# Zeroing the output during attention, smaller routing steps in expert 0, and gates kept in another buffer

## The chip, the cores and the metric

The kernel runs on one core of one Trainium2 chip. The metric is the device time of one execution in microseconds (us); the time before is the median of three runs. A core has a TensorE (PE: matmuls; PEld: its weight loads), a VectorE (DVE), a ScalarE (ACT), a GpSimd (POOL) and a SyncE (SP), which run their own instruction streams in order and wait for each other by semaphores. Transfers issued by SP and by POOL are carried out by 16 DMA engines.

## The reference

Two stages. The first is linear attention with a decaying state, over batch 4, 8 heads, 768 steps, head size 48; for each batch and head:

```
for t: cur = outer(u*k[t], v[t]);  y[t] = r[t] @ (state + cur);  state = w*state + outer(k[t], v[t])
```

The second is a mixture of experts over the 3072 rows x of 384 numbers that y makes: noisy logits for 8 experts, the two largest chosen for each row, their gates a softmax of the two, and

```
noisy = x@w_gate + log1p(exp(x@w_noise))*noise;  top2, gates = softmax over the two largest
out[row] += gate * (relu(x[row] @ w1[e]) @ w2[e])      # 384 -> 1024 -> 384, for both experts e of a row
```

## The kernel before, in words

**Attention** runs over 24 tiles (`for i in range(NT)`, L1223) of 128 rows, 6 chunks of time by 4 batches. In a tile SP loads k, r and v of tile i+4 (`load`, L139) and stores the tile's x to DRAM (`xout`, L485, into `xd`, whose last 8 columns are for the gates); PE makes transposes, scores, y (`intra`, L467; `back`, L476) and, for the tiles before, the logits (`logits`, `logits_b`, L511 to L524).

**Routing** is done by the generator `route(g)` for two groups of rows, tiles 0 to 12 and 13 to 23: some 70 small VectorE steps, among them matmuls on PE for prefix sums (L757) and for a list product (`drop`, L617), which turns one-hot matrices (L604 to L613) into the list of rows for one expert. `one(g, 1)` makes the list for expert 1, `places` and `half` those for experts 2 to 7. The steps are handed out by `rstep(us, pe)`: each call adds `us` to a credit and runs steps of the first one or two generators in the queue while credit is left; a step costs 0.2 unless it yields another price. A step that yields "pe" has a matmul next, which is let go only after a number of `rstep` calls with `pe` true. What is handed out this way stands in the engines' streams between the other work, in this order, for good.

**Experts** come in chunks of up to four tiles of 128 gathered rows: chunk (0,0), (0,1), (1,0) and so on. `xT` transposes gathered rows on PE (L1048), copies them on ACT (L1050: xh, the rounded part) and takes the remainder on DVE (L1051: xl). `p1` makes h for f = 0 to 7 in 9 matmuls each (L1075), copied by ACT (L1079) and DVE (L1081) out of a ring of three PSUM buffers; `p2` makes the output tiles in 24 matmuls each (L1111). Chunk (0,0) uses only rows of the first group, and so starts while the second group is being routed: after each f of p1(0,0) stands one `rstep(STEPS_P1)`, after every 8 matmuls of p2(0,0) one `step00`, which holds an `rstep(STEPS_P2)` and, from step 7 on, the transposes of chunk (0,1), whose rows are gathered (L977) once the second group's list for expert 0 is there. `poll` starts what has become possible: gathers, loads of gates, tokens. If the second group's gates are ready by step AT_ONE, `one(1,1)` is pushed there, else behind p2(0,0). `zero_out` writes 192 rows of zeros to the output (L1295, 16 times), since experts later add to it by gathering and scattering rows (L986, L1132); it stands in the f-loop of p1(0,0) and in `step00`. Then the attention's buffers are freed (`att_stack.close()`), and p1(0,1) begins, with `rstep(0.6)` after each f.

Of the kernel before, what the change touches and what calls it, by code (L numbers as in the profile page):

```python
# [29 lines left out]
STEPS_KV = 0.35  # L30
# [2 lines left out]
FILL = 1  # L33
STEPS_END = 0.9
FLAG_AT = 17
STEPS_P1 = 1.0
STEPS_P2 = 1.4
STEPS_P1B = 0.6
STEPS_P2B = 1.25
WARM1 = 2  # L40
# [5 lines left out]
CV_DVE = 1  # L46
POOL_LATE = 13
BIG = 3.0e38
AT_ONE = 5
NOT = 4  # L50


# [1 line left out]
def kernel(  # L54
# [14 lines left out]
    nc = tc.nc  # L69
    B, H, S, D = r.shape  # L70
    N, E = noise.shape
    DM = H * D
# [55 lines left out]
    def load(i, part=(0, 3)):  # L128
        c, b = divmod(i, B)
        for nm, src, dst in (("kt", k, kt), ("rt", r, rt), ("vt", v, vt))[part[0]:part[1]]:  # L130
            if nm == "rt":
                t = rd[i % NLD][:, :, :D]
            elif nm == "vt":
                t = vd[i % NLD][:, :, :D]
            elif i:
                t = att.tile([128, H, D], F32, name=nm, bufs=NLD - 1)
            else:
                t = kd[0][:, :, :D]
            nc.sync.dma_start(t, src[b, :, c * C:(c + 1) * C, :].rearrange("h t e -> t h e"))  # L139
            dst[i] = t  # L140

    load(0, (0, 2))
    ub = const.tile([128, H, D], F32, name="ub")
# [13 lines left out]
    zrow = const.tile([128, DM], F32, name="zrow")  # L157
# [209 lines left out]
    def prep_k(i, eng=None):  # L367
        for h in (slice(0, H // 2), slice(H // 2, H)):
            (eng or nc.gpsimd).tensor_mul(kd[i % 3][:, h, :D], kt[i][:, h], tabk[:, h, :D])  # L369
# [13 lines left out]
    def uterm_b(i):  # L383
        c8 = att.tile([128, H, 1], F32, name="c8")
        nc.vector.tensor_reduce(c8, RKU[i][:, :, :D // 2 if i > POOL_LATE else D], AX.X, ALU.add)  # L385
        C8[i] = c8
        if i <= CV_DVE:
            CV[i] = att.tile([128, H, D], F32, name="cv")
            nc.vector.tensor_mul(CV[i], vt[i], c8.to_broadcast([128, H, D]))
# [82 lines left out]
    def back(i):  # L472
        pt = psum.tile([128, 2, 2, 2, 64], F32, name="ptb", tag="py1")
        for s in range(2):
            for q in range(2):
                nc.tensor.transpose(pt[:, s, q].rearrange("p j d -> p (j d)"), YB[i][:, s, q, :], ident)  # L476
        PY[i] = pt

    def xout(i):
        x = xs[i % 2]  # L480
        nc.vector.tensor_add(x[:, :DM].rearrange("p (q j s d) -> p (q j) s d", q=2, j=2, s=2),
                             PY[i].rearrange("p s q j d -> p (q j) s d")[:, :, :, :D],
                             CV[i].rearrange("p (q j s) d -> p (q j) s d", q=2, j=2))
        X[i] = x
        nc.sync.dma_start(xd[i * 128:(i + 1) * 128, :], x)  # L485
# [31 lines left out]
    def logits_b(i):  # L517
        if i not in PL:
            return
        pl, ys, m = PL.pop(i)  # L520
        g = [i >= a for a, _ in GROUPS].count(True) - 1
        j = i - GROUPS[g][0]
        nc.tensor.transpose(pl[:, 1, :32 * m], ys[:32 * m], ident[:32 * m, :32 * m])
        nc.scalar.activation(LG[g][:, j - m + 1:j + 1, :],  # L524
                             pl[:, 1, :32 * m].rearrange("p (a b) -> p a b", b=32)[:, :, :2 * E], AF.Copy)
# [32 lines left out]
    def T_of(n):  # L558
        def T(nm, shape=(128, n, E), dt=F32, bufs=1):
            w_ = 1  # L560
            for z in shape[1:]:
                w_ *= z
            mx = w_ // n * GB
            t = att_pool[0].tile([128, mx], dt, name="r_" + nm, bufs=bufs)
            ax = "abcd"[:len(shape) - 1]
            return t[:, :w_].rearrange(f"p ({' '.join(ax)}) -> p {' '.join(ax)}",
                                       **dict(zip(ax, shape[1:])))
        return T
# [98 lines left out]
    def route(g, lists=True):  # L667
        i0, i1 = GROUPS[g]
        n = i1 - i0
# [3 lines left out]
        T = T_of(n)  # L673
# [13 lines left out]
        def P(k, shape=(128, n, E)):  # L687
            w_ = shape[1] * (shape[2] if len(shape) == 3 else 1)
            v = base[:, k * pw:k * pw + w_]
            return v.rearrange("p (a b) -> p a b", b=E) if len(shape) == 3 else v  # L690

        a, ee, zp = P(0), P(1), T("zp")
# [9 lines left out]
        d, s, s2, q, nl, sn = T("n"), P(0), P(2), T("q"), P(0), P(1)  # L702
# [92 lines left out]
        if lists:  # L795
            og = T("os", [128, 2, n, E])
            nc.vector.tensor_mul(og, oh, gts[:, :, :, None].to_broadcast([128, 2, n, E]))
            yield 0.3
            gd = T("a")
            nc.vector.tensor_add(gd, og[:, 0], og[:, 1])  # L800
            nc.sync.dma_start(xd[i0 * 128:i1 * 128, DM:].rearrange("(n p) e -> p n e", p=128), gd)
            yield 0.25
# [355 lines left out]
    def push(*gens, alone=False):  # L1158
        route_q.extend([x, 0, alone] for x in gens)

    def rstep(us, pe=True):

        credit[0] = min(credit[0] + us, us + 0.5)
        if pe:
            for it in route_q[:pairs[0]]:
                it[1] = max(it[1] - 1, 0)
        j = 0
        while j < min(pairs[0], len(route_q)):
            it = route_q[j]
            if it[1] > 0 or (it[2] and j):  # L1170
                j += 1
                continue
            if credit[0] <= 0:
                return
            try:
                c = next(it[0])
            except StopIteration:
                route_q.pop(j)
                j = 0
                continue  # L1180
            if c == "pe":
                it[1] = gap[0]
                credit[0] -= 0.3
            else:
                credit[0] -= c or 0.2
# [32 lines left out]
    def route_when_done(i):  # L1218
        for g, (a, b) in enumerate(GROUPS):
            if b == i + 1:  # L1220
                push(route(g))

    for i in range(NT):  # L1223
        nxt = i + 1 < NT
        if i == 0:
            load(NLD - 1)
        if nxt:
            trans(i + 1, 0)
            uterm_b(i + 1)
            trans(i + 1, 1)  # L1230
        kvup(i)
        inter(i)
        if i > 1:
            logits(i - 2)
        if i + 2 < NT:
            prep_k(i + 2)
            uterm_a(i + 2)
        rstep(STEPS_A, False)
        if i == I_EARLY:
            until(routed, 0)  # L1240
        poll()
        if i == FLAG_AT:
            flag = consts_c()
        if i in (FLAG_AT, FLAG_AT + 2):
            next(flag)
        if not nxt:
            until(gated, 0)
            x00 = xT(0, 0)
            p1a = p1(0, 0, True)
        zadd(i)  # L1250
        intra(i)
        if i > 1:
            logits_b(i - 2)
            route_when_done(i - 2)
        if nxt:
            uterm_c(i + 1, 0, CV_AT)
            scores(i + 1)
            mask(i + 1, 0)
        if i and nxt:
            xtrans(i - 1)  # L1260
        if nxt:
            uterm_c(i + 1, CV_AT, H)
        if not nxt:
            next(x00)
        if i + NLD < NT:
            load(i + NLD)
        if i + 1 in W0_AT:
            w_load(0, W0_AT.index(i + 1))
        back(i)
        xout(i)  # L1270
        if nxt:
            mask(i + 1, 1)
        if i - W_LAG in W0_AT:
            w_hi(0, W0_AT.index(i - W_LAG))
        if i - W_LAG - 1 in W0_AT:
            w_lo(0, W0_AT.index(i - W_LAG - 1))
        rstep(STEPS_KV if nxt else STEPS_END)
    xtrans(NT - 2)
    rstep(STEPS_END)
    next(x00)  # L1280
    xtrans(NT - 1)
    for _ in x00:
        pass
    rstep(STEPS_END)
    logits(NT - 1)
    rstep(STEPS_END)
    fill(FILL)
    pairs[0] = 2
    logits_b(NT - 1)
    route_when_done(NT - 1)  # L1290
    zq = [0]

    def zero_out():
        if zq[0] < N:
            nc.sync.dma_start(out[zq[0]:zq[0] + 192, :].rearrange("(p two) d -> p two d", two=2),  # L1295
                              zrow[:96, None, :].to_broadcast([96, 2, DM]))
            zq[0] += 192

    for whole in p1a:
        if whole:  # L1300
            zero_out()
            rstep(STEPS_P1)
            poll()

    at00 = [0]

    def step00():
        zero_out()
        at00[0] += 1
        rstep(STEPS_P2)  # L1310
        poll()
        if 1 in gated and at00[0] <= AT_ONE and "one" not in did:
            did.add("one")
            push(one(1, 1))
        if "rest" in did and at00[0] > 6:
            next(x01, None)
# [4 lines left out]
    for t in p2(0, 0, step00):  # L1321
        next(wl, None)
        hold.append((0, t))
    while zq[0] < N:
        zero_out()
    until(routed, 1)
    until(gated, 1)
    while route_q:
# [94 lines left out]
    with tc.If(any_r > 0):  # L1423
        bad_r = nc.values_load(tab[:, E:E + 1], min_val=0, max_val=1)
        with tc.If(bad_r > 0):
# [12 lines left out]
            for i in range(NT):  # L1438
                c, b = divmod(i, B)
# [20 lines left out]
        for kk in range(2):  # L1460
# [3 lines left out]
            for i in range(NT):  # L1464
                nc.gpsimd.indirect_dma_start(
                    out=lst, out_offset=bass.IndirectOffsetOnAxis(ap=SLI[:, kk, i:i + 1], axis=0),
# [32 lines left out]
```

## Time and profile before

| what | value |
|---|---|
| time, median of 3 runs | 612.76 us (612.59 to 614.89) |
| profiled execution: its own time, its span | 614.7 us, 612.9 us |
| busy PE, PEld, DVE, ACT, POOL | 577.1, 539.8, 363.3, 252.8, 272.3 us |
| PE in the chain that ended last | 77% of the span (p1's L1075 30%, p2's L1111 29%) |
| mean granted TensorE clock | 0.986 of full speed |
| attention tiles 16 to 23 | about 103 to 147 us of the span |
| p1(0,0), p2(0,0) | 152.8 to 166.4, 166.4 to 185.6 us |
| p1(0,1), p2(0,1) | 186.5 to 206.7, 206.7 to 226.1 us |

Busy time of an engine says little by itself, as the stages have different limits; a row of the timeline gives start, duration, engine, line, operation, output <- inputs, shapes, the number of instructions merged and, in brackets, the idle time of the engine before and what ended it.

### The profile page before, as it was taken

How to read it: one execution, taken by the hardware profiler on the slowest of the kernel's cores; microseconds unless marked ns; L12 is line 12 of the kernel's file. 1: busy time of each engine (PE TensorE's matmuls, PEld its weight loads, DVE VectorE, ACT ScalarE, POOL GpSimd, SP SyncE). 2: the span in 40 equal slices, each digit the busy share in tenths (PEclk: the TensorE clock that was granted, in tenths of full speed). 3: DMA queues.
4: the chain of work that ended last, by engine and by line, in shares of the span. 5: the costliest groups of instructions: out<-in, count | busy, mean ns of one | idle time of the engine just before them, and what ended most of it. 6: DMA issues, size and time to landing. Idle time of an engine off the chain costs nothing.

```text
span 612.9 us, 12600 instructions
## 1 busy us (share of the span) xinstructions
PE 577.1 (94%) x4502; PEld 539.8 (88%) x4503; DVE 363.3 (59%) x858; ACT 252.8 (41%) x639; POOL 272.3 (44%) x413
## 2 busy tenths in 40 slices
PE   7989998997987899999999999999999999999992
PEld 4878887885876899999999999999999999999992
DVE  8647778997784875464365537365553736455320
ACT  2657776664213324343252425244342533434210
POOL 7766686763026036322624453362445226245201
PEclk8989999999999899999999999999999999999997
DMA  8998996625816327453835565374555538354000
GB/s 133 152 225 198 199 198 141 140 59 144 259 49 178 107 61 181 126 166 104 208 102 163 137 167 151 116 203 118 158 139 159 159 106 215 111 161 116 33 19 30
DMA packets 134233, 85.65 MB, mean 140 GB/s; under 512 B 109729, under 2 KB 124289, under 8 KB 134162
## 3 DMA queue, kind: packets, MB, share of 16 engines
q1 hardware_dynamic: 124434, 56.63, 39.1%
q0 software_dynamic: 9728, 28.14, 15.7%
q8 instruction: 37, 0.61, 0.4%
q14 instruction: 34, 0.28, 0.2%
HBM read 58.33 MB, written 19.51 MB: 127 GB/s over the span
## 4 chain that ended last, share of the span: by engine, by line
PE 77%; DVE 10%; SPq 3%; DMA 3%; ACT 2%; issue 2%; another core or an unknown queue 1%; POOL 0%; POOLq 0%; DVEq 0%; ACTq 0%
PE ph L1075 30%; PE pym L1111 29%; PE pa L414 3%; PE yt L467 3%; PE pt L402 2%; SPq L139 1%; PE yt L455 1%; PE pym L1102 1%; PE pym L1104 1%; PE ptx L493 1%; DVE hb L1081 1%; DMA xd<-x 1%; PE pl L511 1%; PE ptb L476 1%
## 5 line engine op out<-in xcount | busy, mean ns | idle before, releaser
L1111 PE MATMUL pym<-w1h,hb 128*128 128x384 f32 x768 | 200.0, 337 | 0.1
L1111 PEld LDWEIGHTS pym<-w1h,hb 128*128 128x128 f32 x768 | 139.0, 188 | 1.1 <-issue 0.5
L1075 PE MATMUL ph<-xh,w0h 128*128 128x384 f32 (+2 forms) x384 | 134.2, 349 | 4.2 <-issue 2.8
L1075 PE MATMUL ph<-xl,w0h 128*128 128x384 f32 (+2 forms) x384 | 133.3, 347 | 0.0
L1075 PE MATMUL ph<-xh,w0l 128*128 128x384 f32 (+2 forms) x384 | 132.9, 346 | 0.0
L1111 PE MATMUL pym<-w1l,hb 128*128 128x384 f32 x384 | 129.1, 336 | 0.8 <-issue 0.8
L1132 POOL DMA_INDIRECT out_dram<-ot,TK x54 | 55.3, 1023 | 158.1 <-DVE ot L1128 121.2
L1081 DVE SCALAR_TENSOR_TENSOR hb<-ph,hb 128x384 fp32r<-128x384 f32 x128 | 71.1, 556 | 91.5 <-ACT hb L1079 37.5
L1079 ACT ACTIVATE hb<-ph 128x384 fp32r<-128x384 f32 x128 | 62.9, 492 | 108.1 <-PE ph L1075 84.9
L1075 PEld LDWEIGHTS ph<-xh,w0h 128*128 128x128 f32 x384 | 72.5, 189 | 7.4 <-issue 3.4
L1075 PEld LDWEIGHTS ph<-xh,w0l 128*128 128x128 f32 x384 | 72.6, 189 | 1.4
L1075 PEld LDWEIGHTS ph<-xl,w0h 128*128 128x128 f32 x384 | 72.6, 189 | 1.3 <-DVE xl L1051 0.2
L1111 PEld LDWEIGHTS pym<-w1l,hb 128*128 128x128 f32 x384 | 72.1, 188 | 0.5 <-issue 0.5
L977 POOL DMA_INDIRECT xgt<-xd,GR x40 | 42.2, 1056 | 63.8 <-DVE hb L1081 17.5
L986 POOL DMA_INDIRECT pv<-out_dram,GA x47 | 53.4, 1136 | 27.7 <-issue 15.1
L1117 ACT ACTIVATE ot<-pym 128x384 f32<-128x384 f32 x39 | 19.1, 491 | 92.4 <-PE pym L1111 67.5
L1051 DVE TENSOR_TENSOR xl<-xq,xh 128x384 fp32r<-128x384 f32 (+2 forms) x40 | 21.2, 531 | 43.5 <-ACT xh L1050 30.0
L396 ACT ACTIVATE cv<-vd,c 128x48 f32<-128x48 f32 x176 | 44.0, 324 | 1.5 <-DVE c L385 1.3
L421 DVE TENSOR_TENSOR am<-pa,mneg 128x512 int32<-128x512 int32 x48 | 32.8, 684 | 16.5 <-PE pa L414 16.4
L369 POOL TENSOR_TENSOR kd<-kt,tabk 128x192 f32<-128x192 f32 x46 | 27.1, 609 | 22.0 <-DMA kt<-in_k_dram 17.8
L1050 ACT ACTIVATE xh<-xq 128x384 fp32r<-128x384 f32 (+2 forms) x40 | 20.0, 500 | 33.8 <-DVE xq L1041 19.6
L1128 DVE SCALAR_TENSOR_TENSOR ot<-ot,GT,pv 128x384 f32<-128x384 f32 (+2 forms) x44 | 26.4, 610 | 11.8 <-ACT ot L1117 11.8
(294 smaller groups left out, 812.5 us busy)
## 6 DMA issues: line engine op xcount, KB each, us to landing
stg<-in_moe_w_dram SPq DMA_DIRECT2D x32, 384.0 KB
stg<-in_moe_w_dram SPq DMA_DIRECT2D x72, 128.0 KB
xq<-xgt SPq DMA_DIRECT2D x172, 36.0 KB
xd<-x SPq DMA_DIRECT2D x24, 196.0 KB
rd<-in_r_dram SPq DMA_DIRECT2D x24, 192.0 KB
vd<-in_v_dram SPq DMA_DIRECT2D x24, 192.0 KB
out_dram<-zrow SPq DMA_DIRECT2D x16, 288.0 KB
kt<-in_k_dram SPq DMA_DIRECT2D x23, 192.0 KB
```

The lines of the kernel that those rows point to most:

```text
L369: (eng or nc.gpsimd).tensor_mul(kd[i % 3][:, h, :D], kt[i][:, h], tabk[:, h, :D])
L396: nc.scalar.activation(CV[i][:, h, :], vt[i][:, h, :], AF.Copy, scale=C8[i][:, h, :])
L421: nc.vector.tensor_tensor(AM[i][:, s].bitcast(I32), PA[i][s].bitcast(I32), mneg.to_broadcast([128, NP, 128]), op=ALU.bitwise_and)
L977: nc.gpsimd.indirect_dma_start(out=xg[:n], out_offset=None, in_=xd[:GROUPS[GEARLY - 1][1] * 128] if early_ else xd, in_offset=bass.Indirec ...
L986: nc.gpsimd.indirect_dma_start(out=pv[:n], out_offset=None, in_=out, in_offset=bass.IndirectOffsetOnAxis(ap=GA[:n, e * NJ + t:e * NJ + t + ...
L1051: nc.vector.tensor_sub(xl[:, g], v, xh[:, g].bitcast(F32))
L1075: nc.tensor.matmul(ph[:, :w_], a[:, d, fs], x[:, :w_ // 32, d], start=(j == 0), stop=(j == len(q) - 1))
L1079: nc.scalar.activation(h_[:, f, 0, :], ph[:, a:b], AF.Relu)
L1081: nc.vector.scalar_tensor_tensor(h_[:, f, 1, :], ph[:, a:b], 0.0, h_[:, f, 0, :].bitcast(F32), op0=ALU.max, op1=ALU.subtract)
L1111: nc.tensor.matmul(py, hb[:, f, a, hs], x[:, f, :], start=(j == 0), stop=(j == len(q) - 1))
L1128: nc.vector.scalar_tensor_tensor(ot[:n], pt[:n], g, PV[e, t][:n], op0=ALU.mult, op1=ALU.add)
L1132: st = nc.gpsimd.indirect_dma_start(out=out, out_offset=bass.IndirectOffsetOnAxis(ap=TK[:n, q:q + 1], axis=0), in_=ot[:n], in_offset=None, ...
```

## The change

The zero writes go from p1(0,0) and p2(0,0) into attention tiles 16 to 23, two a tile, behind the loads and ahead of the store of x. The steps of routing in p1(0,0) and p2(0,0) are smaller (0.85 and 1.2), AT_ONE is 4. In the last tile and behind it `rstep` is called with `pe` false, so that no matmul of a list is let go there, and `logits_b` of tile 21 stands behind `back`. The gates that are stored to xd are added into the space of u's copy `ub` and not into the buffer `r_a`.

```diff
@@ -33,8 +33,8 @@
 FILL = 1
 STEPS_END = 0.9
 FLAG_AT = 17
-STEPS_P1 = 1.0
-STEPS_P2 = 1.4
+STEPS_P1 = 0.85
+STEPS_P2 = 1.2
 STEPS_P1B = 0.6
 STEPS_P2B = 1.25
 WARM1 = 2
@@ -46,7 +46,8 @@
 CV_DVE = 1
 POOL_LATE = 13
 BIG = 3.0e38
-AT_ONE = 5
+AT_ONE = 4
+ZERO_AT = 16
 NOT = 4
 
 
@@ -796,7 +797,7 @@
             og = T("os", [128, 2, n, E])
             nc.vector.tensor_mul(og, oh, gts[:, :, :, None].to_broadcast([128, 2, n, E]))
             yield 0.3
-            gd = T("a")
+            gd = ub.rearrange("p h d -> p (h d)")[:, :n * E].rearrange("p (a b) -> p a b", b=E)
             nc.vector.tensor_add(gd, og[:, 0], og[:, 1])
             nc.sync.dma_start(xd[i0 * 128:i1 * 128, DM:].rearrange("(n p) e -> p n e", p=128), gd)
             yield 0.25
@@ -1220,6 +1221,14 @@
             if b == i + 1:
                 push(route(g))
 
+    zq = [0]
+
+    def zero_out():
+        if zq[0] < N:
+            nc.sync.dma_start(out[zq[0]:zq[0] + 192, :].rearrange("(p two) d -> p two d", two=2),
+                              zrow[:96, None, :].to_broadcast([96, 2, DM]))
+            zq[0] += 192
+
     for i in range(NT):
         nxt = i + 1 < NT
         if i == 0:
@@ -1249,7 +1258,7 @@
             p1a = p1(0, 0, True)
         zadd(i)
         intra(i)
-        if i > 1:
+        if i > 1 and nxt:
             logits_b(i - 2)
             route_when_done(i - 2)
         if nxt:
@@ -1264,9 +1273,14 @@
             next(x00)
         if i + NLD < NT:
             load(i + NLD)
+        if i >= ZERO_AT:
+            zero_out()
+            zero_out()
         if i + 1 in W0_AT:
             w_load(0, W0_AT.index(i + 1))
         back(i)
+        if not nxt:
+            logits_b(i - 2)
         xout(i)
         if nxt:
             mask(i + 1, 1)
@@ -1274,38 +1288,28 @@
             w_hi(0, W0_AT.index(i - W_LAG))
         if i - W_LAG - 1 in W0_AT:
             w_lo(0, W0_AT.index(i - W_LAG - 1))
-        rstep(STEPS_KV if nxt else STEPS_END)
+        rstep(STEPS_KV if nxt else STEPS_END, nxt)
     xtrans(NT - 2)
-    rstep(STEPS_END)
+    rstep(STEPS_END, False)
     next(x00)
     xtrans(NT - 1)
     for _ in x00:
         pass
-    rstep(STEPS_END)
+    rstep(STEPS_END, False)
     logits(NT - 1)
-    rstep(STEPS_END)
+    rstep(STEPS_END, False)
     fill(FILL)
     pairs[0] = 2
     logits_b(NT - 1)
     route_when_done(NT - 1)
-    zq = [0]
-
-    def zero_out():
-        if zq[0] < N:
-            nc.sync.dma_start(out[zq[0]:zq[0] + 192, :].rearrange("(p two) d -> p two d", two=2),
-                              zrow[:96, None, :].to_broadcast([96, 2, DM]))
-            zq[0] += 192
-
     for whole in p1a:
         if whole:
-            zero_out()
             rstep(STEPS_P1)
             poll()
 
     at00 = [0]
 
     def step00():
-        zero_out()
         at00[0] += 1
         rstep(STEPS_P2)
         poll()
@@ -1321,8 +1325,6 @@
     for t in p2(0, 0, step00):
         next(wl, None)
         hold.append((0, t))
-    while zq[0] < N:
-        zero_out()
     until(routed, 1)
     until(gated, 1)
     while route_q:
```

## Rows read from the trace of the kernel before

**Rows 1.** Chain that ended last, in order of time: start us, us, what.
```profile
253.43 14.71 PE ph L1075 x72
...
394.07 12.49 PE ph L1075 x72
```

**Rows 2.** Waits of TensorE, 138 to 226 us: total us, times, longest us.
```profile
PE pwarm L617 <- DVE r_ob L613: 4.7, 3, 2.4
```

**Rows 3.** Timeline of TensorE, 140 to 227 us.
```profile
152.42 0.47 PE L617 MATMUL pwarm<-r_ob,r_oa 128*128 128x14 bf16 x13 [2.37 <-DVE r_ob L613]
...
166.37 0.34 PE L1111 MATMUL pym<-w1h,hb 128*128 128x384 f32 x1
...
169.17 0.20 PE L757 MATMUL pwarm<-r_om,ltri 128*128 128x88 bf16 x1 [1.24 <-DVE r_om L750]
...
173.37 0.42 PE L617 MATMUL pwarm<-r_ob,r_oa 128*128 128x14 bf16 x11 [0.84 <-DVE r_ob L613]
...
182.69 0.42 PE L617 MATMUL pwarm<-r_ob,r_oa 128*128 128x14 bf16 x11 [1.53 <-DVE r_ob L613]
...
184.73 0.82 PE L1048 MATMUL ptm<-ident,xg 128*128 128x128 f32 x6
...
186.49 0.47 PE L1075 MATMUL ph<-xh,w0h 128*128 128x448 f32 x1 [0.94 <-ACT xh L1050]
...
199.06 0.44 PE L1075 MATMUL ph<-xh,w0h 128*128 128x448 f32 x1 [2.82 <-issue]
...
206.74 0.33 PE L1111 MATMUL pym<-w1h,hb 128*128 128x384 f32 x1
...
212.45 0.66 PE L617 MATMUL pwarm<-xgt 128*128 128x84 bf16 x13 [1.40 <-DVE xgt L613]
...
226.13 0.34 PE L1075 MATMUL ph<-xh,w0h 128*128 128x384 f32 x1
```

**Rows 4.** Timeline of VectorE, 144 to 232 us.
```profile
150.60 1.01 DVE L1051 TENSOR_TENSOR xl<-ptm,xh 128x384 fp32r<-128x384 f32 x2
...
156.16 0.15 DVE L679 TENSOR_SCALAR ie_n<-pwarm 128x1 f32<-128x1 f32 x1
...
173.05 0.26 DVE L613 TENSOR_SCALAR r_ob<-r_ob,pcol 128x77 bf16<-128x77 bf16 x1
...
198.22 0.56 DVE L1081 SCALAR_TENSOR_TENSOR hb<-ph,hb 128x384 fp32r<-128x384 f32 x1 [3.71 <-PE ph L1075]
...
202.87 1.22 DVE L344 TENSOR_TENSOR w0l<-stg,w0h 128x1024 fp32r<-128x1024 f32 x1
...
205.57 1.08 DVE L604 TENSOR_TENSOR xgt<-r_mm,im 128x896 bf16<-128x896 int32 x1
...
212.03 0.37 DVE L613 TENSOR_SCALAR xgt<-xgt,pcol 128x546 bf16<-128x546 bf16 x1
```

**Rows 5.** Timelines of GpSimd and of SP's DMA issues, 100 to 232 us.
```profile
103.20 0.39 SPq L139 DMA_DIRECT2D kt<-in_k_dram  x1
...
175.93 0.94 POOL L977 DMA_INDIRECT xg<-xd,GR  x1 [21.80 <-DVE f L819]
...
179.66 0.92 POOL L977 DMA_INDIRECT xg<-xd,GR  x1 [0.30 <-issue]
...
182.76 0.39 SPq L801 DMA_DIRECT2D xd<-r_a  x1
```

**Rows 6.** Timeline of ScalarE, 128 to 232 us.
```profile
197.59 0.49 ACT L1079 ACTIVATE hb<-ph 128x384 fp32r<-128x384 f32 x1 [6.18 <-PE ph L1075]
```

**Rows 7.** Stretches: length, busy PE, PEld, DVE, ACT, POOL (instructions); PEclk, DMA share, GB/s.
```profile
115.00:120.00 5.00, 5.00 (x82) 4.31 (x80) 4.79 (x15) 3.63 (x14) 3.97 (x8) 1.00 0.76 158
...
148.00:156.00 8.00, 5.52 (x49) 4.54 (x50) 4.69 (x14) 1.91 (x6) 2.91 (x3) 1.00 0.89 246
...
156.00:166.00 10.00, 9.95 (x56) 9.43 (x55) 9.28 (x39) 2.95 (x6) 0.00 (x0) 1.00 0.97 306
...
200.00:202.00 2.00, 2.00 (x7) 1.64 (x6) 0.85 (x5) 1.49 (x5) 0.00 (x0) 0.50 0.29 84
```

## The prediction

> **What bounds the kernel now.** I read the table of busy time by stage first, then the waits of TensorE, the chain, and the timelines of TensorE and VectorE from the last attention tile to the second chunk of expert 1. From about 230 us on, TensorE is busy in every slice and the chain is a row of matmul blocks: 72 matmuls of 448 columns in 14.71 us (0.204 each), 72 of 384 columns in 12.49 us (0.173 each) [rows 1]. A change to routing can win nothing there; it only moves the start. Between 150 and 226 us TensorE waits, and what ends nearly every wait is VectorE, on which the routing of the second token group and the lists stand: 4.7 us in three products of lists for the first experts [rows 2], 1.40 us for a product of the later lists and 1.24 us for the prefix sums [rows 3]. VectorE runs without a gap from 156.16 to 173.31, 17.15 us [rows 4]. So each routing step that stands too early in TensorE's stream is paid as a wait.
>
> **The change, part by part.**
>
> *Which step stands where* is counted from the code: each routing step draws its cost from the credit of a slot. With slots of 1.0 and 1.4 the prefix sums stand at step 1 of the nine steps (8 matmuls each) of p2(0,0), the list product of expert 0 at step 3, the gates at 5; the list of expert 1 is pushed at step 5 (5 <= AT_ONE) and its product stands at step 8. With 0.85 and 1.2 they stand at steps 2, 5 and 7, and the list of expert 1, no longer due by step 4, goes behind p2(0,0), into p1(0,1), its product at f=5. TensorE's rows show the old places: 169.17, 173.37, 182.69 [rows 3].
>
> *Last tile.* The product at 152.42 waited 2.37 us [rows 3]. It goes behind the first f of p1(0,0); what is late next is xl, done at 150.60 + 1.01 = 151.61 [rows 4], so 0.8 us come back, and the product's 0.3 us is paid later. Moving logits_b(21) behind back(23) lets three transposes start up to one us earlier, but back(23) still waits for its own copy; I cost it at nothing (bounds: -0.3 to +0.2). VectorE starts the second group's routing about 1.1 us earlier, at 155.05.
>
> *p1(0,0) and p2(0,0).* TensorE: 3 + 6 + 63 matmuls from 151.61 with 0.7 us of small products between end near 164.9 (before: p2 began at 166.37 [rows 3]). 16 matmuls (2.8) to 167.7; the prefix sums wait for VectorE until 169.1 - 1.1 = 168.0, and take 0.4. 24 matmuls (4.2) to 172.6: the list product. VectorE is done at 155.05 + 17.15 = 172.2, so the old 0.84 us is gone. From that product to the first gather of x for chunk (0,1) it took 175.93 - 173.37 = 2.56 us; one more step stands between (0.2): gather at 175.35. Gathers follow each other by (179.66 - 175.93)/3 = 1.24, and the store behind the last one was let go 182.76 - 179.66 = 3.1 us after its start [rows 5]; I take 3.1 as the time to landing. So x lands at 178.45, 179.7, 180.9 and 182.2.
> TensorE is at step 7, where the first transposes of that x stand, at 172.6 + 0.3 + 16 x 0.173 = 175.7, and waits 2.7 us: **the new wait**, in place of 1.24, 0.84 and 1.53. Then two times 8 matmuls (1.4) and transposes (0.35) bring the last transposes to 182.2. In the profile p1(0,1) began 186.49 - 184.73 = 1.76 us after them [rows 3]; so it begins at 183.9 or so, **2.6 us earlier**.
>
> *p1(0,1) and p2(0,1).* The list of expert 1 adds its product here (+0.35) and about 4 us of VectorE. The product of the next lists moves from step 3 to step 6 of p2(0,1). VectorE's queue, counted from the start of p1(0,1): first remainder of h at 2.65; eight of them with their tails at 0.6 (0.56 for the large part [rows 4]) 4.8; list of expert 1 3.2; rows and tokens 1.9; ranks 1.8; four remainders of weights at up to 1.22 [rows 4] 4.6; gaps 0.5; makes 19.5. Then places 1.9, the two halves of a one-hot 1.9 (1.08 the larger [rows 4]), two steps 1.4, two xl 1.0, the last step 0.37 [rows 4]: ready at 26.0 (an estimate; the terms without a row of their own are from rows of the same kind). TensorE is there after 72 x 0.204 + 0.4 + 48 x 0.173 + 0.6 = 24.0. The old wait of 1.40 [rows 3] becomes 2.0, but the third product of this stage (0.44) goes to the next.
> In the profile there is one more loss: ScalarE's copy of f=2 starts at 197.59 though its matmuls were done at 192.6; TensorE then stands 2.82 us and runs at 1.2 GHz behind that (199.06; clock 0.50 [rows 3, 6, 7]). Both stages took 226.13 - 186.49 = 39.64. No row explains this stall of some 5.5 us. If it stays, VectorE catches up behind it (it stood 3.71 us [rows 4]) and the list wait vanishes: p1 +0.35, p2 -1.4 - 0.44. If it is in neither execution, VectorE would have been ready at 212.40 - 3.71 = 208.7 and TensorE there at 212.45 - 1.40 - 5.5 = 205.5: the old list product would have waited 3.2, the new one waits 2.0, p1 +0.35, p2 -1.2 - 0.44. Either way -1.3 to -1.5, and +0.44 in the next stage. What follows (gathers for chunk (1,1), list for expert 2 at 240 rather than 231 us) has over 9 us until its first user.
>
> *Zeroed output.* 16 writes of 288 KB move from p1(0,0) and p2(0,0) to tiles 16 to 23, two a tile. In 156 to 166 us, mostly such writes, 306 GB/s took 0.97 of the engines [rows 7]; so two writes are 0.59 MB / 0.306 = 1.9 us of all of them; eight tiles between 103.2 [rows 5] and the end of the last near 147 have 5.5 us each, of which this is a third (0.34). The fullest of these tiles stand at 0.76 [rows 7]: with it they are over-full. Cover: loads run four tiles ahead, in the queue before the writes; the store of x stands behind them, and its buffer is needed two tiles later. I take 0; bounds -0.5 (a free queue at 148 to 163) to +7.6, four loading tiles each longer by 1.9.
> The Trainium skill, "DMA: Bandwidth & Descriptors", section "Issuing engines are not separate DMA queues", says that transfers run on the same 16 engines and interleave whoever issues them; the gathers and loads would feel the writes. By it the writes are not free in tiles 16 to 19, which is the slower rival below; by the lead of the loads they are.
>
> *Gates in u's space.* The same add, to another place, u's last reader being done by 133 us. It takes a wait away only from a tile that lies over the old buffer; I see none in the rows: 0 (bounds -1 to +0.2).
>
> **Sum:** -2.6 - 1.4 + 0.44 = -3.56, taken as -3.5. The profiled execution took 614.7 (span 612.9 and 1.8 around it), 1.9 over the median of 612.76; so 611.2 for one like it. As both readings of the stall give nearly the same difference, I take it from the median: **609.3**.
>
> **Rivals.**
> 1. *The stall goes too.* If the late copy of f=2 is bound to what stands around it (scatters, gathers and weights of the same moment), a p1(0,1) with other neighbours loses it, and 5.5 less 2.1 for the list wait that returns comes on top: 605.8. For: it happens once in 128 such copies. Against: no row says what makes it.
> 2. *The clock eats the gain.* The new wait of 2.7 us lies between one of 2.37 us, after which the clock stayed at 2.4 GHz (clock 1.00 in 148 to 156), and the one of 2.82 us, after which it fell to 1.2 GHz (0.50) [rows 3, 7]. The 27 matmuls after 199.06 took 7.68 us for 5.5: about 1.8 lost. On which side 2.7 falls no row says. If the clock falls: 609.3 + 1.8 = 611.1. The Trainium skill, "TensorE: Matmul & The Clock Gate", section "Part 1: The HAM clock gate", has it that the half rate is the default and activity lifts it; the trace agrees (0.50 behind the pause).
> 3. *Slower: the writes starve attention.* Place: tiles 16 to 19, which load and now write. If the engines' share passes 1, loads come later by 1.9 a tile, and once the lead of a load (kt is asked for two tiles ahead) is used up, TensorE waits: four tiles, 7.6 less 1 of lead: 609.3 + 6.6 = 615.9. For: 0.76 + 0.34 is over 1. Against: 0.76 is the fullest tile, and a load has two tiles of lead before the lateness reaches anyone.
> 4. *Nothing.* The gathers alone set p1(0,1)'s start and land as late as before: 612.7.
>
> **How the numbers follow.** Forecast 0.42 (own range 607.6 to 611.0), rival 1 0.20, rival 2 0.25, rival 3 0.08, rival 4 0.05. The range runs from rival 1 to behind rival 4: 605.0 to 613.0, leaving out the slower rival and tails. 0.5% (3.06 us) is what a measurement here tells from no change: faster is below 609.70. The forecast gives 0.25 of its 0.42 to it, rival 1 all, rival 2 0.02: 0.47. Slower: rival 3 and 0.01: 0.09. The rest 0.44.
>
> **What would show it.** TensorE's waits for the one-hots of the first lists (4.7) nearly gone; a wait of 2 to 3 us before the transposes of x at p2(0,0) step 7, ended by a gather; p1(0,1) beginning near 184; the list of expert 1 inside p1(0,1); the lists' product waiting about 2 us near 208. A clock of 0.5 near 180 is rival 2; no 2.8 us stop in p1(0,1) is rival 1; tiles 16 to 19 longer than 5.5 us, or GpSimd waiting for kt, is rival 3. Wrong altogether if the list of expert 1 still stands in p2(0,0), or if the gathers land over 3.5 us after their start.

## The result and the profile after

The changed kernel takes **607.24 us** (median of 6 runs, 605.91 to 611.11) beside 613.05 for the kernel before in the same hours: a ratio of **0.9908, 95% interval 0.988 to 0.9937**, some 5.6 us less. Forecast were 609.3 and 3.5 us less; the time lies inside the range (605.0 to 613.0) and 0.4 us below the forecast's own range (607.6 to 611.0). On chip C of the experiments below it was 605.78 beside 610.65, 0.9933 (0.9905 to 0.9961). The profiled execution of the changed kernel is its longest, 611.11 us with a span of 609.2, so its total is not the median's; its stages can be compared, and of the 3.6 us between the two profiled executions (614.7 and 611.11) each stage's share can be read. All lines of the code up to the zero writes are one further down than in the kernel before.

TensorE's waits between 130 and 226 us; they answer to [rows 2]:

```profile
PE ptm L1049 <- DMA xg<-xd,GR: 3.4, 3, 2.6
PE pwarm L679 <- DVE L L622: 1.4, 1, 1.4
PE pwarm L618 <- DVE xgt L614: 1.3, 1, 1.3
PE ph L1076 <- DVE xl L1052: 1.1, 1, 1.1
PE ph L1076 <- ACT xh L1051: 0.9, 1, 0.9
PE ptb L477 <- ACT yb L471: 0.9, 1, 0.9
PE pwarm L618 <- DVE xq L614: 0.6, 1, 0.6
```

The 4.7 us for the one-hots of the first lists are gone, and so is the "issue" of 2.8 us. Two waits are new: the transposes of gathered x (2.6, forecast 2.7), and one that the forecast did not have, the column sums with which the second group's routing begins (L679, 1.4). TensorE's timeline shows where; it answers to [rows 3]:

```profile
149.83 0.44 PE L1076 MATMUL ph<-xl,w0h 128*128 128x384 f32 x1 [1.09 <-DVE xl L1052]
151.74 0.48 PE L618 MATMUL pwarm<-r_ob,r_oa 128*128 128x14 bf16 x13
153.61 0.17 PE L679 MATMUL pwarm<-acc,ones_b 128*128 128x8 bf16 x1 [1.39 <-DVE L L622]
...
164.70 0.34 PE L1112 MATMUL pym<-w1h,hb 128*128 128x384 f32 x1
167.78 0.20 PE L758 MATMUL pwarm<-r_om,ltri 128*128 128x88 bf16 x1
172.38 0.43 PE L618 MATMUL pwarm<-r_ob,r_oa 128*128 128x14 bf16 x11
178.31 0.55 PE L1049 MATMUL ptm<-ident,xg 128*128 128x128 f32 x3 [2.62 <-DMA xg<-xd,GR]
180.38 0.84 PE L1049 MATMUL ptm<-ident,xg 128*128 128x128 f32 x3
183.38 0.82 PE L1049 MATMUL ptm<-ident,xg 128*128 128x128 f32 x6
185.14 0.47 PE L1076 MATMUL ph<-xh,w0h 128*128 128x448 f32 x1 [0.94 <-ACT xh L1051]
197.15 0.42 PE L618 MATMUL pwarm<-xq 128*128 128x14 bf16 x11 [0.59 <-DVE xq L614]
201.19 0.33 PE L1112 MATMUL pym<-w1h,hb 128*128 128x384 f32 x1
220.75 0.34 PE L1076 MATMUL ph<-xh,w0h 128*128 128x384 f32 x1
```

p2(0,0) runs from 164.70, p1(0,1) from 185.14, p2(0,1) from 201.19, p1(1,0) from 220.75; before they began at 166.37, 186.49, 206.74 and 226.13. The windows answer to [rows 7]: tiles 16 to 19 with the writes, and the stretch behind the gather's wait, where the mean granted clock, third number from the right, lies between the two levels, 1.2 GHz being 0.50 and 2.4 GHz 1.00:

```profile
115.00:120.00 5.00, 5.00 (x81) 4.31 (x83) 4.83 (x15) 3.62 (x12) 3.98 (x8) 1.00 0.96 223
...
176.00:184.00 8.00, 5.70 (x28) 5.41 (x28) 3.49 (x16) 1.07 (x3) 2.93 (x4) 0.79 0.44 95
```

ScalarE's copies in p1(0,1) answer to [rows 6]. The one of f=2 is on time, the one of f=3 starts 2.4 us behind its matmuls (their end: 192.91):

```profile
191.12 0.49 ACT L1080 ACTIVATE hb<-ph 128x384 fp32r<-128x384 f32 x1 [1.22 <-PE ph L1076]
...
195.33 0.49 ACT L1080 ACTIVATE hb<-ph 128x384 fp32r<-128x384 f32 x1 [2.65 <-PE ph L1076]
```

**A measure that lets traces be compared.** The end of attention lies up to 6.6 us apart in the fourteen traces, so I count from the first transpose of the last tile's `back` (L476, L477 after; 146.29 us before, 144.76 after). Every number in this table is a difference of two starts in TensorE's timeline, in the last two columns of the span's end and a start. B, C and D are three chips; A stands for the pair above, whose chip is not on record, so that it may be one of the three. The changed kernel has no trace on B or D, nor has the kernel before. Each row is one execution: e2 and e4, for one, have 2.5 us in p1(0,0) from a lower clock that e1, with nearly the same waits there, does not have.

| kernel, chip | back to p2(0,0) | back to p1(0,1) | p1(0,1) and p2(0,1) | p1(1,0) to the end | back to the end |
|---|---|---|---|---|---|
| before, A | 20.1 | 40.2 | 39.6 | 386.8 | 466.6 |
| changed, A | 19.9 | 40.4 | 35.6 | 388.5 | 464.4 |
| before again (r1), C | 21.1 | 41.1 | 39.6 | 387.1 | 467.8 |
| changed again (r2), C | 19.9 | 40.3 | 35.6 | 386.9 | 462.7 |
| e1 zeros back, B | 19.8 | 40.2 | 33.9 | 385.8 | 459.9 |
| e2 steps back, B | 22.3 | 42.0 | 34.0 | 384.9 | 460.9 |
| e3 steps alone, B | 21.2 | 38.4 | 33.8 | 386.2 | 458.4 |
| e4 list inside, B | 22.3 | 42.7 | 34.1 | 385.8 | 462.6 |
| x2 product at step 4, C | 20.1 | 37.8 | 34.3 | 387.6 | 459.6 |
| x3 and column sums first, C | 18.5 | 36.3 | 35.8 | 387.1 | 459.1 |
| s1 scatters later, D | 19.9 | 40.1 | 41.2 | 385.6 | 466.9 |
| x4 = x3 and scatters later, D | 18.5 | 36.2 | 34.3 | 389.1 | 459.7 |
| c2 steps back, D | 19.9 | 39.7 | 39.9 | 388.1 | 467.7 |
| c3 steps alone, D | 22.4 | 39.4 | 34.3 | 388.7 | 462.3 |

So of the gain, 4.0 us are in p1(0,1) and p2(0,1), on A and on C; the start of p1(0,1), which should have brought 2.6, brought -0.2 on A and 0.8 on C, and there r1's p1(0,0) took 1.0 longer than that of the kernel before on A (14.62 beside 13.62), at a lower clock.

### The profile page after: what moved, and what is told of

Its sections match the earlier page's. It is cut to its first block, busy times and chain, and to the rows that moved or that the text cites. A ratio compares the mean times of both kernels' runs of the same rounds, so it can differ in the third digit from the quotient of the medians.

```text
span 609.2 us, 12597 instructions
## 1 busy us (share of the span) xinstructions
PE 576.6 (95%) x4502; PEld 539.7 (89%) x4503; DVE 366.0 (60%) x858; ACT 253.0 (42%) x639; POOL 272.0 (45%) x413
## 4 chain that ended last, share of the span: by engine, by line
PE 83%; DVE 10%; DMA 3%; ACT 2%; issue 1%; POOL 0%; POOLq 0%; DVEq 0%; ACTq 0%
PE ph L1076 33%; PE pym L1112 31%; PE pa L415 3%; PE yt L468 3%; PE pt L403 2%; PE pym L1105 1%; PE pym L1103 1%; PE yt L456 1%; PE ptx L494 1%; DMA xg<-xd,GR 1%; PE pwarm L431 1%; PE ptb L477 1%; DVE am L422 1%; PE pl L512 1%; DVE hb L1082 1%
## 5 line engine op out<-in xcount | busy, mean ns | idle before, releaser
L422 DVE TENSOR_TENSOR am<-pa,mneg 128x512 int32<-128x512 int32 x48 | 32.7, 683 | 14.6 <-PE pa L415 14.4
L370 POOL TENSOR_TENSOR kd<-kt,tabk 128x192 f32<-128x192 f32 x46 | 28.4, 638 | 18.4 <-DMA kt<-in_k_dram 13.5
L1051 ACT ACTIVATE xh<-xq 128x384 fp32r<-128x384 f32 (+2 forms) x40 | 20.0, 500 | 33.8 <-DVE xq L1042 17.6
```

The source lines that it names most:

```text
L422: nc.vector.tensor_tensor(AM[i][:, s].bitcast(I32), PA[i][s].bitcast(I32), mneg.to_broadcast([128, NP, 128]), op=ALU.bitwise_and)
```

## The experiments

**Four parts, each undone or done alone (chip B).** There the kernel before takes 603.68 us, so the absolute numbers that I had expected, written for A, are to be read against that.

e1, the writes back where they were:

```diff
-        if i >= ZERO_AT:
-            zero_out()
-            zero_out()
...
         if whole:
+            zero_out()
             rstep(STEPS_P1)
...
     def step00():
+        zero_out()
         at00[0] += 1
```

> The changed kernel with one part undone: the sixteen zero writes stand again in p1(0,0) and p2(0,0); the smaller steps, the last tile and the gates' place stay. My theory (the gain comes from where the routing steps stand; the writes cost nothing in attention and held nothing up in the experts): about 607.5 us, within 1.5 of the changed kernel's 607.2; p1(0,1) begins within 0.7 us of where it does in the changed kernel and takes 16 to 17 us. Rival A (the writes were in the way of the gathers, weights or scatters round p1(0,1), and the 2.8 us stop of TensorE there went with them): 610 to 612.5, a stop of 2 us or more in p1(0,1) again. Rival B (the writes cost attention time now): 605 to 606.5, tiles 16 to 23 shorter.

Measured 601.88, 0.9974 (0.9952 to 0.9996). p1(0,1) begins as late behind the back as in the changed kernel (40.2), with the same wait for the gather (2.55) and the same clock (0.79); there is no stop in p1(0,1) though the writes stand in p1(0,0) and p2(0,0) again. That does not yet rule out rival A, since no kernel traced on B has the stop; c2 and c3, below, do it on D, where the stop is there with the writes in attention and not with the writes in the experts. From tile 16's back to tile 23's it takes 38.18 us without the writes, 38.26 with them (e2, same chip): rival B falls.

e2 and c2 (the same kernel, on B and on D), the sizes of the steps undone:

```diff
-STEPS_P1 = 0.85
-STEPS_P2 = 1.2
+STEPS_P1 = 1.0
+STEPS_P2 = 1.4
...
-AT_ONE = 4
+AT_ONE = 5
```

> The changed kernel with the sizes undone: steps of 1.0 and 1.4 and AT_ONE 5, so the prefix sums, the list product of expert 0 and the gates stand at steps 1, 3 and 5 of p2(0,0) and the list of expert 1 inside it, as before; the writes, the last tile and the gates' place stay changed. My theory: only the 0.8 to 1.1 us of the last tile remain, so 612 us (611 to 612.7); TensorE waits again 1 to 1.5 us at each of the three products in p2(0,0). Rival A (the stop in p1(0,1) went with the writes): 608 to 609.5, the waits in p2(0,0) back but p1(0,1) about 16.5 us long. Rival B (the gain is in the last tile): 607 to 608.

> The changed kernel with steps of 1.0 and 1.4 and AT_ONE 5 once more, now beside kernels whose traces show where the copies of p1(0,1) are late. If the sizes of the steps carry the change: within 1.5 us of before where that shows the stop (610 to 613), with a copy 4 to 6 us late in p1(0,1). If the writes or the last tile do: 4 to 5.5 us below it, no such copy.

e3 and c3 (on B and on D) are the kernel before with 0.85, 1.2 and AT_ONE 4, and nothing else:

> The kernel before with the sizes alone: steps of 0.85 and 1.2 and AT_ONE 4; the writes stand in p1(0,0) and p2(0,0), the list product of expert 1's first group in the last tile, the gates in r_a. My theory: 608.5 us (607.5 to 609.8), that is all but the 0.8 to 1.1 us of the last tile. Rival A (writes): 610 to 612 with the stop in p1(0,1). Rival B (last tile): 612 to 613.

> The kernel before with steps of 0.85 and 1.2 and AT_ONE 4 once more, beside the same kernels. In its trace the list product stood at step 4 of p2(0,0), not 5 as in the changed kernel, the gather's wait was 0.2 us and from the first gather to p1(0,1) it took 8.3 us. My theory: that again, no copy more than 2.5 us late, and a ratio to before of 0.983 to 0.988, that is faster than the changed kernel's 0.993. Rival (the writes in attention or the last tile carry the change): 0.997 to 1.0.

On B: e2 602.53, 0.9979 (0.9963 to 0.9996); e3 602.77, 0.9977 (0.996 to 0.9993). Both gain little (0.9 to 1.2 us), and no trace of B has a late copy in p1(0,1): all four take 33.8 to 34.1 us for p1(0,1) and p2(0,1). That the kernel before has none there either, and so had little to lose, is a guess: it was not traced on B. The clock of p1(0,0) in the traces of e1 and then of e2 (third number from the right) shows how far two executions can differ with nearly the same waits of TensorE at its start (1.24 us in both, then 0.93 and 0.89); p1(0,0) took 16.07 and 18.55 us:

```profile
150.00:156.00 6.00, 6.00 (x37) 6.00 (x36) 5.22 (x19) 1.97 (x4) 0.00 (x0) 1.00 0.96 297
150.00:156.00 6.00, 6.00 (x28) 6.00 (x28) 3.94 (x17) 0.98 (x2) 0.00 (x0) 0.74 0.01 5
```

On D: c2 610.1, 0.9939 (0.9908 to 0.997), c3 607.89, 0.9925 (0.9897 to 0.9953), beside 612.93. Both expectations missed in part: c2 gained more than the 1.5 us that the theory of the step sizes allows, c3 less than 0.983 to 0.988, and their intervals overlap, so that the times alone do not tell the parts apart; the traces do. In c2, which has the writes in attention, the new last tile and the gates in `ub`, the stretch behind the last back takes as long as in the kernel before and in s1 (467.7 us beside 466.6 to 467.8), the stop included. TensorE's waits, then ScalarE's copy of f=2, whose matmuls ended at 186.61:

```profile
PE ph L1076 <- remote: 4.4, 1, 4.4
PE pwarm L618 <- DVE r_ob L614: 2.2, 2, 1.5
```

```profile
193.16 0.49 ACT L1080 ACTIVATE hb<-ph 128x384 fp32r<-128x384 f32 x1 [7.73 <-remote]
```

c3, with the step sizes alone, has neither: 462.3 us from the back to the end, 34.3 in the two stages. So behind the last tile the gain is that of the step sizes, as far as one trace of each shows. What c2 gains beside that lies ahead of the back, which begins at 140.82 there, at 144.28 in c3 and at 142.15 in s1; I come to it at the end. Of what c3 lacks to its expectation, the trace shows that late back and a p1(0,0) of 15.93 us at a lower clock. And c3 and e3 show something that neither kernel of the case has. Their list product stands at step 4 of p2(0,0), not 5, because without the new last tile more credit is left over. TensorE's timeline of c3:

```profile
173.50 0.42 PE L617 MATMUL pwarm<-r_ob,r_oa 128*128 128x14 bf16 x11 [0.65 <-DVE r_ob L613]
178.37 0.55 PE L1048 MATMUL ptm<-ident,xg 128*128 128x128 f32 x3 [0.18 <-DMA xg<-xd,GR]
183.63 0.47 PE L1075 MATMUL ph<-xh,w0h 128*128 128x448 f32 x1 [0.93 <-ACT xh L1050]
```

A short wait for VectorE (0.65) in place of a long one for the gather, and from the first gather (175.37) to p1(0,1) it takes 8.26 us; in the changed kernel 185.14 - 175.17 = 9.97.

e4, AT_ONE 9, so that expert 1's list is pushed at step 7 of p2(0,0):

```diff
-AT_ONE = 4
+AT_ONE = 9
```

> The changed kernel with AT_ONE 9: the list of expert 1 is pushed at step 7 of p2(0,0), its product stands behind the last step of p2(0,0) and not in p1(0,1), and the products of the later lists stand at steps 3, 6 and 9 of p2(0,1) again. My theory (putting this list off is worth something by itself): TensorE waits at that product for 3 us of VectorE's steps, of which the transposes and the gather's wait cover half: p1(0,1) begins 1 to 2 us later, p2(0,1) waits 1.5 to 2.5 more for its first list, so 609 to 611. Rival (the smaller steps of the second group alone carry the gain, and it is one where this list stands): 607.2, within 1.

603.32, 0.9987 (0.9973 to 1.0001); not settled. The product did not wait where I expected it (p2(0,0) took 20.34, as in e1: the gather's lateness covers it); what e4 has more than e1 in its trace, 2.5 us, lies in p1(0,0), where its clock was at 0.66 from 150 to 156 us, as in e2.

**Both kernels again, on one chip (C).**

> The kernel before, unchanged, once more for its trace: on the chip of the four runs above it takes 603.7 us and not 613. My theory now: the late copy of f=2 in p1(0,1), with the stop of TensorE behind it, belongs to the chip or the execution and not to the program; here p1(0,1) takes 15.0 to 15.5 us and p1(0,1) with p2(0,1) some 34 to 36 us instead of 39.64, and from the last tile's back to the end there are 460 to 462 us instead of 466.6. Rival (the program makes the stop, by its zero writes, weights and scatters of that moment): a copy 4 to 6 us behind its matmuls again, and 39 to 40 us.

> The changed kernel, unchanged, beside the kernel before on a chip on which that one takes 603.7 us. My theory now (4 of the 5.6 us were the stop in p1(0,1), which is not the program's): 601.5 to 602.7, a ratio of 0.996 to 0.9985. The recorded sum (-2.6 for the start of p1(0,1) and -1.4 behind it, on every chip): 600.2, 0.994. If the gain were all the program's: 598, 0.991.

My theory of that moment, that the stop belongs to chip or execution, falls by half (its ratio for r2 was 0.996 to 0.9985, that of the recorded sum 0.994). r1 (one run, 611.73) has the stop at the same f=2: TensorE's waits, and ScalarE's copy, whose matmuls ended at 189.31:

```profile
PE pwarm L617 <- DVE r_ob L613: 4.8, 3, 2.4
PE ph L1075 <- issue: 3.4, 1, 3.4
```

```profile
194.93 0.49 ACT L1079 ACTIVATE hb<-ph 128x384 fp32r<-128x384 f32 x1 [6.81 <-issue]
```

r2 (605.78, 0.9933) has the copy of f=3 late by 2.36 us, where A had 2.42. So the same program has it at the same place in both pairs, and no kernel traced on B has one.

**The product one step earlier (x2) and the column sums first (x3), on C.**

```diff
-STEPS_P2 = 1.2
+STEPS_P2 = 1.25
```

> The changed kernel with one number different: steps of 1.25 and not 1.2 in p2(0,0), which puts the list product of expert 0 at step 4 and not 5; all else stands where it was. My theory (at step 5 the product comes after VectorE was ready, the gathers start late, TensorE waits 2.6 us for them and then runs for some us at 1.2 GHz): the product waits 0.3 to 1.3 us for VectorE, the first gather starts 0.5 to 0.9 us earlier, the wait for it falls below 1 us, the clock stays at 1.00, and from the first gather to p1(0,1) it takes 8.3 us and not 9.9: 2 to 2.5 us less than the changed kernel. Rival (VectorE bounds the whole stage, so the wait only changes its place): within 0.5 us of the changed kernel.

600.79, **0.9831 (0.9808 to 0.9854)**: 5.0 us less than the changed kernel. TensorE's timeline:

```profile
167.91 0.42 PE L618 MATMUL pwarm<-r_ob,r_oa 128*128 128x14 bf16 x11 [0.65 <-DVE r_ob L614]
173.26 0.55 PE L1049 MATMUL ptm<-ident,xg 128*128 128x128 f32 x3 [0.66 <-DMA xg<-xd,GR]
175.03 0.49 PE L1049 MATMUL ptm<-ident,xg 128*128 128x128 f32 x3
176.75 0.82 PE L1049 MATMUL ptm<-ident,xg 128*128 128x128 f32 x6
178.51 0.47 PE L1076 MATMUL ph<-xh,w0h 128*128 128x448 f32 x1 [0.94 <-ACT xh L1051]
```

and the window behind the wait, with the clock:

```profile
172.00:180.00 8.00, 6.39 (x38) 5.43 (x37) 3.92 (x15) 2.16 (x5) 2.27 (x3) 1.00 0.48 102
```

The wait is 0.66, the clock 1.00, and from the first gather (170.18) to p1(0,1) it takes 8.33 us. p1(0,1) begins 2.5 us earlier behind the back, as expected; another 1.3 come from p1(0,1) and p2(0,1), where the copy of f=3 is late by 0.5 and not 2.4, which I had not expected. So of the 5.0 us the product's place is shown to bring 2.5.

x3 adds this, around the last tile:

```diff
         if not nxt:
+            gap[0] = 2
             until(gated, 0)
...
+    gap[0] = 1
     for whole in p1a:
```

> The one before this with one more edit: the list product of expert 1's first group is let go one slot later, behind f=1 of p1(0,0), so the column sums with which the second group's routing begins stand ahead of it. My theory (in the changed kernel that matmul waits 1.4 us for VectorE to read the product out of the same PSUM tile, and so VectorE's routing, which bounds the stage, starts 1.4 us late): that wait goes, the routing starts 1.0 to 1.4 us earlier after the last tile's back, p1(0,1) too; 1 to 1.4 us less than the kernel without this edit. Rival (TensorE's 72 matmuls of p1(0,0) bound the stage, or the wait moves to the product at f=1): within 0.4 us of it.

600.94, 0.9827 (0.9807 to 0.9847). The mechanism was right: the sums stand ahead of the product and wait for nothing,

```profile
149.04 0.18 PE L679 MATMUL pwarm<-acc,ones_b 128*128 128x8 bf16 x1
150.73 0.48 PE L618 MATMUL pwarm<-r_ob,r_oa 128*128 128x14 bf16 x13
```

and p1(0,1) begins 1.5 us earlier (36.3). The time did not follow: the copy of f=3 is late by 2.43 again, and the two stages take 35.8.

**Is it the scatters? (s1 and x4, on D.)** The late copies stand where GpSimd issues the scatters of chunk (0,0), so I moved these, in the kernel before (s1) and in x3 (x4):

```diff
-            while hold:
+            while hold and (s > 1 or j > 4):
                 emit_out(*hold.pop(0))
```

> The kernel before with one thing moved: the three scatters of chunk (0,0)'s output are issued behind f=5 of p1(0,1), not behind f=0; GpSimd's gathers for chunk (1,0) then stand ahead of them. Theory S (the scatters, which GpSimd issues between 4.8 and 8.9 us after the start of p1(0,1), hold up the semaphore by which ScalarE and VectorE learn that TensorE's f=2 is done): no copy over 1 us late at f=2 to 4, no stop of TensorE, p1(0,1) takes 15 to 15.5 us and not 20.3, the time is 3.5 to 4.5 us below the kernel before, if that shows the stop in the same hours (610 to 613 us). Theory C (the chip, or a transfer of another kind): the copy of f=2 is 4 to 6 us late again and the time is within 1.5 us of before.

> The fastest candidate: smaller steps of 1.25, the column sums ahead of the list product of expert 1's first group, and the scatters of chunk (0,0) behind f=5 of p1(0,1). Theory S: the copy of f=3, 2.4 us late without this edit, is on time, and p1(0,1) with p2(0,1) take 34 us and not 35.8, so 599.3 where the kernel without it takes 600.9 (a ratio to before of 0.980 to 0.9815). Theory C: 600.9, 0.9827, or a later start of the next gathers makes it 0.5 us slower.

s1: 612.73, 1.0001 (0.9972 to 1.003). Theory S falls: the copy of f=2 (matmuls done at 188.30) is late by 8.1 us.

```profile
196.36 0.49 ACT L1079 ACTIVATE hb<-ph 128x384 fp32r<-128x384 f32 x1 [9.24 <-remote]
```

GpSimd's rows in that time, gathers now ahead of scatters:

```profile
181.87 0.94 POOL L1021 DMA_INDIRECT GT<-xd,GX  x1 [5.54 <-DMA xd<-r_a]
...
186.93 0.95 POOL L977 DMA_INDIRECT xg<-xd,GR  x1 [0.39 <-issue]
...
193.83 0.98 POOL L1132 DMA_INDIRECT out_dram<-ot,TK  x1 [0.24 <-issue]
```

x4: 603.47, 0.9847 (0.9807 to 0.9888), no better than x3. Its f=3 is only 0.5 late, but so it is in c3, where the scatters were not moved; and f=6 and f=7 of p1(1,0) are late by 2.3 and 4.4 (in c3 by 1.7 and 4.4). x2, x3 and x4 are the fastest versions; which of them, their intervals do not tell.

## Why the prediction came out, step by step

**Right: which step stands where.** Prefix sums, list product and gates stand at steps 2, 5 and 7, the list of expert 1 at f=5 of p1(0,1).

**Right: the writes cost nothing.** Tiles 16 to 23 take 39.35 us from back to back, before 39.36, while the share of the DMA engines in 115 to 120 us rose from 0.76 [rows 7] to 0.96. Rival 3 has no trace in the rows. That transfers of all queues share the engines (the Trainium skill, "DMA: Bandwidth & Descriptors", section "Issuing engines are not separate DMA queues") does not speak against it: the loads run ahead, and the tiles show no wait for what they may have lost.

**Wrong: "p1(0,1) begins 2.6 us earlier".** Two terms of it failed. The first is the last tile: 1.5 us were to be won up to p2(0,0), 0.1 were (20.1 to 19.9). I let the product go behind the first f and costed what stands behind it at nothing; but the column sums write to the PSUM tile out of which VectorE must first read the product, and waited 1.39. In x3, where they stand ahead, p2(0,0) begins 1.6 us earlier than in x2 (18.5 beside 20.1 behind the back). The second is the clock. The new wait came as forecast (2.62), and rival 2, with its chance of 0.25, came with it: in all four traces that have a gather wait of 2.5 to 2.6 us the clock fell (0.79 in the eight microseconds around it in each). Its price of 1.8 was well sized: 9.97 us from the first gather to p1(0,1) beside 8.33 in x2. The times of the steps in p2(0,0), 167.78, 172.38 and 175.17 beside 168.0, 172.6 and 175.35, look right and are not: attention ended 1.5 us earlier in that execution, and counted from the back they are 1.3 late.

**Wrong: "both stages -1.4, however one reads the stall".** They lost 4.0, and not where the sum had it: p1(0,1) went from 20.25 to 16.05 us, where 0.35 more was forecast, and p2(0,1) from 19.39 to 19.56, where 1.6 to 1.8 less was. Each of my readings kept the stop or left it out on both sides; what happened is the mechanism of rival 1, in part: the late copy shrank from 5.0 to 2.4 us, and since TensorE has three PSUM buffers, 2.4 makes it stand only 0.59 us, at the list product, whose one-hots VectorE makes behind that copy, where 5.0 made it stand 2.82. The list wait in p2(0,1) is 1.34, hardly less than the 1.40 before (forecast 2.0, or none if the stall stayed), and a wait of 0.42 for a gather is new there. p1(1,0) takes 14.22 and not 13.79, the 0.44 that the forecast put there. That the late copy "happens once in 128" was a misreading: the kernel before has a second one, of 1.06 us, at f=2 of p1(1,0), and f=3 of p1(0,1) is late behind the first.

**So that the total was near is in part luck**: two terms failed by 2.8 and 2.6 us in opposite directions, rivals 1 and 2 at once. The forecast treated them as cases of which one happens; they are in different stages and exclude nothing. In the profiled pair, 3.6 us apart, they make -3.8: +0.2 up to p1(0,1) and -4.0 in the two stages. The rest is +1.7 from p1(1,0) on, of which 0.4 was forecast and 1.1 stands in one later stage, around a copy that is 1.9 us late there, and -1.5 ahead of the last back, where the forecast had nothing: the gates' place, which it put at 0 with bounds of -1 to +0.2, is the part that may have failed there (below).

**What is shown of the late copies, and what is not.** In ten traces on A, C and D, all 30 copies of h that start over 0.4 us behind their matmuls, with ScalarE free, have matmuls that end within a row of six or more indirect DMAs that GpSimd issues one behind the other (0.75 us between them at most), or at most 0.1 us behind it. Where the row in p1(0,1) has ten (before, r1, s1, c2: the list of expert 1 is done early, so the gathers for chunk (1,0) join gates and scatters), f=2 is late by 5.0 to 8.1; where it has seven (changed, r2, x2, x3, x4, c3), f=3 by 0.5 to 2.4. That is what the smaller steps changed: the next gathers start at 200.70 and not 195.68, outside the row. That the length of the row makes the difference is argued from this and not shown. But B, with rows of ten as well (e2, e4), has none, and rows of ten behind 330 us have none on any chip. The semaphore is late itself and not its reader: VectorE's own wait for it ends in the moment in which ScalarE's copy starts (197.59 us in the kernel before, 196.36 in s1, 195.33 in the changed kernel). What delays it stays open; breaking up the row with pauses was not tried.

**Also open: the start of attention.** Up to tile 16 both kernels issue the same instructions in the same order; yet the last back comes at 139.7 to 142.1 us on B, C and D in the eight executions with the gates in `ub`, and at 142.1 to 145.7 in the four with `r_a` (144.76 and 146.29 on A). Most of the difference is at tile 4, where VectorE waits for the store of an earlier tile's x, up to 3.5 us, and TensorE for VectorE: 6.3 to 7.4 us from back to back beside 7.1 to 11.4 (9.5 and 10.1 on A). It shows earlier still. From 10 to 15 us the share of the DMA engines is 0.90 to 0.97 in all nine traces with the gates in `ub` and 1.15 to 1.31 in all five with `r_a`, A and B among them, for about as many GB/s. On D, c2 and then c3 (second number from the right):

```profile
10.00:15.00 5.00, 3.76 (x57) 3.06 (x57) 4.93 (x10) 1.36 (x3) 5.00 (x9) 1.00 0.90 138
10.00:15.00 5.00, 3.57 (x57) 3.10 (x57) 4.93 (x9) 1.36 (x3) 5.00 (x9) 1.00 1.15 140
```

So this part seems to belong to the program and not to the execution. e1 excludes the writes as its cause, and c2 the sizes of the steps. Of what is left only the gates' place changes a buffer (`r_a` is no longer made), and with it perhaps where others lie; that is argued, for it was not tried by itself. It would be why c2 is below before (0.9939) though the stretch behind the back is as long, and it may be a good part of what the change gained.

## What to carry to other kernels

Compare traces from a common event just ahead of the change, not from the start: absolute times agreed with the forecast here and hid two wrong terms. A matmul that starts a gather is placed by two waits, its own and that of the gather's first reader: at step 5 it waited for nothing and cost 2.6 us and the clock later, at step 4 it waited 0.65 and p1(0,1) began 2.5 us earlier. Rivals in different stages can all come true, so their prices are to be added up as well as weighed against each other. A part that is forecast at nothing needs its own experiment too: the gates' place, which was not undone alone, is the one that stays open here.

## What the hardware showed unexpectedly

- TensorE's semaphore arrived up to 8 us late (s1, f=2), at ScalarE and VectorE at once, while TensorE went on; in all ten traces of A, C and D, beside rows of indirect DMAs, and in none of the four of B.
- A wait of the same length did not settle the clock: behind the 2.37 to 2.40 us ahead of p1(0,0) it stayed at 1.00 in two executions (before, s1) and fell in three (r1, e3, c3; 0.50 from 152 to 156 us in c3), where p1(0,0) then took 14.6 to 15.9 us for 13.5 to 13.6. In the changed order it stayed at 1.00 behind a wait of 1.24 us in e1 and fell to 0.50 (148 to 152 us) behind the same wait in e2.
- The same kernel before takes 603.7 us on chip B and 610.7 and 612.9 on C and D (613.1 in the pair above); the four variants that ran on B gained 0.4 to 1.8 us there.
- In 10 to 15 us, with the same instructions issued, the DMA engines' share is 1.15 to 1.31 in the five traces with `r_a` and 0.90 to 0.97 in the nine without; why is open.
